# First loads of a four-layer attention kernel issued from two queues instead of one

## The chip, the core and the metric

The kernel runs on one core of a Trainium2 chip. Five engines work side by side and meet through semaphores: TensorE (PE in the profile, with its weight loads as PEld), VectorE (DVE), ScalarE (ACT), GpSimd (POOL) and SyncE (SP). Transfers between HBM and the core's memory are issued by an engine's sequencer (SPq, ACTq in the profile) and carried out by 16 DMA engines. The metric is device time in microseconds of one execution; lower is better.

## The reference

`x` is 2048 tokens of 512 values in bf16. Four residual layers follow each other, A, B, A, B. Only A's beginning matters here.

```python
def _A_ref(x, wqkv, w_phi, wo):                 # H = 32 heads of Dh = 16
    q, k, v = split_heads(x @ wqkv)
    pq = einsum("bhsd,hdf->bhsf", q, w_phi)     # one 16x16 matrix for each head
    pk = einsum("bhsd,hdf->bhsf", k, w_phi)
    phi_q = concat([softmax(pq), softmax(-pq)])
    phi_k = concat([softmax(pk), softmax(-pk)])
    kv  = einsum("bhsf,bhsd->bhfd", phi_k, v);  z = phi_k.sum over s
    num = einsum("bhqf,bhfd->bhqd", phi_q, kv)
    den = einsum("bhqf,bhf->bhq", phi_q, z) + 1e-6
    return merge_heads(num / den) @ wo

def _B_ref(x, wqkv, wo):                        # 8 earlier tokens at a stride of 2
    ...

x = x + _A_ref(layernorm(x), A_wqkv, A_w_phi, A_wo)
x = x + _B_ref(layernorm(x), B_wqkv, B_wo)
x = x + _A_ref(layernorm(x), A_wqkv, A_w_phi, A_wo)
x = x + _B_ref(layernorm(x), B_wqkv, B_wo)
```

## The kernel before

The tokens lie in four blocks of 512 (`x[0]` to `x[3]`, x0 to x3 in the text), each of four tiles of 128 tokens. All weights are held on the core. The matrices of `w_phi` are multiplied into the q and k parts of `wqkv` once, at the start ("fold"), so that layer A's first products give `pq` and `pk` at once.

The kernel is written as many small steps, each for one engine. `_ORDER`, a list of numbers, says which step is played next, and every engine then runs its instructions in that order; a solver made the list, and the tables of buffers (`_SLOTS`) with it. An engine that waits for something holds up everything behind it in its own order.

The head, up to about 14 us, is this:

- `s_loads` issues the loads. The four tiles of x0 come one by one (`lx0`, L337), x1 to x3 whole (`lx`, L340). The third part of `wqkv`, for v, goes straight to `WA` (`lv`, L343). The k and q parts go to raw buffers, `wraw`, each in two halves of 256 columns (`lraw`, L349); `qk` is 1 for k and 0 for q, `h` is the half. Then come pieces of the output weights `WoA` (L353), and layer B's `WB` and `WoB` (L418, L422). All of these are issued by SP. `w_phi` (`phis`, L325) is issued by ACT in `setup`, ahead of all steps.
- A DMA signals one of eight semaphores, handed out in turn in the order of the list over both queues. So a DMA's issue waits until the one eight before it has landed, and what stands behind it on that engine waits too.
- `s_fold`: PE transposes half of a raw part with eight products against the identity (`tr`, L386), DVE or ACT copies the result to `wT` (L202 is the copy on DVE, L204 on ACT), PE multiplies it with the block-diagonal `PHI` (`mm`, L396: 16 products of 128 columns for each part), and ACT copies four results to `WA` (L204, "CAST WA"). The part for k comes first, that for q after it.
- LayerNorm of x0: statistics of a tile on DVE (L515, L516), logarithm and exponential on ACT (L450, L453), the shift on DVE (L457, `nmr`), the tile itself on ACT (L468) or DVE (L466), transposes on PE (L482), copies on ACT.
- Then layer A's dense products: L632 for k (four products of 512 columns that add up, one for each row block of `WA`, so the fourth needs the last of the four casts), L644 for v, L737 for q; ACT takes exponentials from their results (L638 `Ek`, L745 `Eq`).
- `warm` (L309): products of a zero tile with itself, whose result nobody reads. Eleven come first on PE, two after the transposes of the first half of k, one after the transposes of the first tile of x0.
- `c_ind_av` (L268, `indAV`) is one of several small constants that DVE makes at the start.

On PE the order of the head is: eleven products of zeros; transposes of the first half of k; two products of zeros; transposes of the second half of k; transposes of x0's first tile; one product of zeros; transposes of the first half of q; then L396 for k with x0's second tile among them; transposes of the second half of q; L632.

Of the kernel before, what the change touches and what calls it, by code (L numbers as in the profile page):

```python
# [23 lines left out]
NB = 4  # L24
# [20 lines left out]
    "fold_dma": (),  # L45
    "half_k": ((0, 3), (1, 3)),
# [5 lines left out]
    "warm": 14,  # L52
# [8 lines left out]
8 2 i 2e 2p 23 i a i i 9 i i i i i i i 4e 1m i 0 0 f i e c j b 2 k 3 4 j o 1m l 3 m p 1n 0 i 1 n 1t o 1o q 1m 1p  # L61
r 0 1m 1u s 1m z z z 5 1m 1r 7 6 z 20 20 7 1q 1s 1t 21 21 t 20 20 1v 22 10 z 22 1t 7 1t 20 1w 22 t 11 24 24 13 u
12 16 12 1t t 15 1t v 12 12 22 x 18 14 1x d w w 1y 2c y 18 18 26 18 2d 1f 2d 2c 1z 2d 24 2d 27 17 19 18 1a 1b 21
1c 1d 22 21 22 39 1e 20 20 22 39 25 2c 3b 3a 3a 1f 3a 2d 3a 2f 2c 1f 1f 39 22 2f 2d 2g 1g 29 1f 2d 1j 2f 2d 7 1h
29 1i 1k 3a 29 2n 29 2i 2n 3c 2o 2o 2o 2k 2o 2k 2q 1l 2h 2n 2a 2k 2f 2n 2k 3a 2o 2j 24 2q 2r 2q 2o 2o 2o 29 2y
28 2y 2y 3c 2l 2z 2v 2z 2s 2z 2z 2k 2y 2z 39 36 31 2z 36 2z 3a 3b 36 36 2v 31 2v 37 2v 31 2t 36 2z 36 2b 2b 2b
2b 2m 2m 36 36 2m 3a 2w 2m 2v 33 34 32 31 3c 35 2q 3c 36 3b 2x g 2x 2u 2x 30 37 2x 36 38 38 38 38 3i 3c 3h 3c 39
3b 3a 3j 3k 3k 3k 3c 3d 3c 3e 3l 3b 3m 3d 3e 5h 3n 3m 3c 3e 3e 3l 5i 3o 3m 3q 3p 3m 3m 4f 3r 3m 3d 3l 5j 3e 3e
3s 3m 5i 3t 3m 3u 3m 3v 3d 3e 3e bd 5h 5m 5n 5k 5i 5l 5i 5i 3m 3d 3e 7c 5h 7d 5p 5i 5o 5i 5i 5r 3f 3g 3g 5q 5i
3f 3g 5i 3w 3f 3z 3x 3f 3g 5s 3y 7e 40 41 3g 7d 5u 5v 7f 5t 3g 41 42 41 41 44 3g 43 3g 43 5w 5x 5x 7f 45 46 43  # L70
43 47 43 7f 5y 3f 90 47 48 49 3g 4c 91 5x 41 4b 41 41 41 4a 92 5x 4d 60 91 4l 5z 61 5z 93 5z 4q 62 5z 4g 7d 4g
4g 4m 4q 63 5z 7d 4r 93 4i 4l 63 66 64 67 7g 4s 7j 65 7h 7i 4h 4j 7k bo 4n 4q 4q 4u 4w 91 7l 4t 7l 7l 7m 7l 7o
68 7n 7n 4l 7p 3h 7n 7q 4w 93 4v 7n 4v 91 4f 6a 7r 4o 6b 7n 6k 6f 69 4g 4k 4l 7r 6l 7s h 4w 6g 6k 6m 4p 6a 6c 6p
# [37 lines left out]

_SLOTS = {
    "med": (
        "b79ca642352f85de6b0464b12833892cb7516e70efd8561f1706ed4a53bc7430e3f9eba731d9c0411a4091d20483b8ae4cf4"
        "b71d6236f9ec40bfd6ea7830c4"
    ),
    "ps": (
# [19 lines left out]
class _Fast:  # L137
# [193 lines left out]
    def s_loads(self):  # L331
# [23 lines left out]
        for t in range(4):  # L355
            add("ld_x0", "SP", lx0, t)
# [1769 lines left out]
```

## Time and profile before

| | us |
|---|---|
| median of 3 runs | 319.39 (319.31 to 320.0) |
| profiled execution | 319.68 |
| its span | 317.9 |
| PE, DVE, ACT busy in the span | 307.5, 295.1, 275.2 |
| transfers, first 30 us | 6.87 MB, mean 229 GB/s |

In the profile's rows a group is given by line, engine, operation and output and input tiles. In the timeline the columns are start, length, engine, line, operation, and in brackets the engine's idle time just before and what ended it. In the rows of windows, the numbers after the stretch are its length and the busy time of PE, PEld, DVE, ACT and POOL with the count of instructions, then PE's granted clock, the DMA engines' share and GB/s. "To landing" is the time from a DMA's issue to its last semaphore increment. In the rows of DMA queues, q1 is SP's queue and q10 is ACT's; the columns are packets, MB and the time that the packets took as a share of 16 engines.

### The profile page before, as it was taken

Reading aid. Unit: us, or ns where it says so; the run is one execution under the profiler, and the core shown is the slowest. Engines: PE = TensorE matmul, PEld = TensorE weight load, DVE = VectorE, ACT = ScalarE, POOL = GpSimd, SP = SyncE. Lnnn points to the kernel's source line nnn. Section 1 sums busy time; section 2 is a strip of 40 time slices with the busy share of each in tenths; the row PEclk is TensorE's granted clock in tenths of the full one; section 3 lists DMA queues with packets and bytes.
Section 4 is the critical chain, followed back from the end, with each engine's and each line's share of the span. In section 5 each row is a group of like instructions: output and inputs, shape, how many; then the busy total and the mean of one; then the engine's idle time right before and its main releaser. Section 6 shows DMA issues by size and latency. Waiting matters only on the chain.

```text
span 317.9 us, 8896 instructions
## 1 busy us (share of the span) xinstructions
PE 307.5 (97%) x3578; PEld 153.0 (48%) x3578; DVE 295.1 (93%) x459; ACT 275.2 (87%) x639; POOL 47.1 (15%) x60
## 2 busy tenths in 40 slices
PE   8999999899999999999999999988999999999994
PEld 4654456445454444444444455544454544444552
DVE  6999996898999999999999999699998999999994
ACT  3999999999888778999999999899999867788761
POOL 6000000000003212000000000027011644045000
PEclk9999999999999999999999999999999999999999
DMA  6986200005694989569895500005189885565954
GB/s 199 345 203 143 41 2 4 2 19 142 150 191 96 157 141 139 99 106 151 140 131 71 69 0 2 4 19 134 49 195 137 134 157 119 103 181 122 163 148 170
DMA packets 45789, 36.37 MB, mean 114 GB/s; under 512 B 30832, under 2 KB 41136, under 8 KB 45744
## 3 DMA queue, kind: packets, MB, share of 16 engines
q1 hardware_dynamic: 45216, 35.75, 56.5%
q8 instruction: 29, 0.48, 0.7%
q14 instruction: 16, 0.13, 0.2%
q10 hardware_dynamic: 528, 0.02, 0.1%
HBM read 11.13 MB, written 3.25 MB: 45 GB/s over the span
## 4 chain that ended last, share of the span: by engine, by line
PE 88%; ACT 5%; DVE 2%; DMA 2%; SPq 1%; issue 1%; DVEq 0%; ACTq 0%
PE PS L967 23%; PE PS L553 18%; PE PS L632 9%; PE PS L644 9%; PE PS L737 6%; PE PS L1128 4%; PE PS L1066 4%; PE PS L1185 2%; DMA wraw<-in_A_wqkv_dram 2%; PE PS L707 2%; ACT Eq L745 2%; PE PS L482 1%; PE PS L940 1%; PE PS L556 1%; PE PS L1200 1%; PE PS L1082 1%
## 5 line engine op out<-in xcount | busy, mean ns | idle before, releaser
L967 PE MATMUL PS<-xnT,WB 128*128 128x512 bf16 x336 | 76.6, 380 | 0.0
L1059 DVE TENSOR_TENSOR prod<-QT,K 128x4096 bf16<-128x4096 bf16 x28 | 63.3, 2285 | 0.5 <-POOL K L993 0.5
L1121 DVE TENSOR_TENSOR pav<-PT,Vg 128x4096 bf16<-128x4096 bf16 (+1 forms) x29 | 62.9, 2213 | 0.2
L967 PEld LDWEIGHTS <-WB 128*128 128x128 bf16 x336 | 37.3, 114 | 36.3 <-issue 3.1
L745 ACT ACTIVATE Eq<-PS 128x512 bf16<-128x512 f32 x64 | 36.3, 619 | 0.0
L638 ACT ACTIVATE Ek<-PS 128x512 bf16<-128x512 f32 x64 | 35.1, 623 | 0.2 <-PE PS L632 0.2
L553 PEld LDWEIGHTS <-oT 128*128 128x128 bf16 x236 | 21.9, 98 | 26.6 <-issue 1.3
L737 PE MATMUL PS<-xnT,WA 128*128 128x512 bf16 x128 | 32.0, 380 | 0.5 <-DVE s L829 0.3
L578 ACT ACTIVATE sqd<-x 128x512 bf16<-128x512 bf16 x48 | 30.0, 635 | 2.1 <-DVE x L571 2.0
L644 PE MATMUL PS<-WA,xnT 128*128 128x512 bf16 x128 | 31.6, 379 | 0.0
L571 DVE SCALAR_TENSOR_TENSOR x<-PS,x 128x512 bf16<-128x512 f32 x46 | 30.1, 683 | 0.7 <-PE PS L553 0.7
L632 PE MATMUL PS<-WA,xnT 128*128 128x512 bf16 x128 | 30.7, 379 | 0.0
L204 ACT CAST oT<-PS 128x512 bf16<-128x512 f32 (+1 forms) x50 | 26.8, 600 | 3.6 <-PE PS L1128 2.1
L553 PE MATMUL PS<-WoA,oT 128*128 128x512 bf16 x128 | 29.8, 380 | 0.0
L553 PE MATMUL PS<-WoB,oT 128*128 128x512 bf16 x108 | 26.5, 379 | 0.0
L204 ACT CAST K<-PS 128x512 bf16<-128x512 f32 x30 | 17.3, 594 | 3.0 <-PE PS L967 1.9
L632 PEld LDWEIGHTS <-xnT 128*128 128x128 bf16 x128 | 12.4, 98 | 14.8 <-issue 0.4
L644 PEld LDWEIGHTS <-xnT 128*128 128x128 bf16 x128 | 12.3, 98 | 14.4 <-issue 0.4
L690 DVE TENSOR_TENSOR Ek<-Ek,rk 128x4096 bf16<-128x4096 bf16 (+1 forms) x10 | 18.6, 1859 | 0.4 <-ACT rk L685 0.4
L737 PEld LDWEIGHTS <-WA 128*128 128x128 bf16 x128 | 11.7, 98 | 14.6 <-issue 1.7
L466 DVE TENSOR_SCALAR xn<-x,rstd,nmr 128x512 bf16<-128x512 bf16 x48 | 17.5, 412 | 0.5
L204 ACT CAST V<-PS 128x512 bf16<-128x512 f32 x26 | 15.2, 596 | 2.9 <-PE PS L967 2.9
(175 smaller groups left out, 506.4 us busy)
## 6 DMA issues: line engine op xcount, KB each, us to landing
Vg<-V SPq DMA_DIRECT2D x112, 131.5 KB, 4.7
Prho<-rd SPq DMA_DIRECT2D x8, 512.0 KB, 5.3
x<-in_A_x_dram SPq DMA_DIRECT2D x3, 512.0 KB, 6.8
WB<-in_B_wqkv_dram SPq DMA_DIRECT2D x3, 512.0 KB, 9.6
out_dram<-x SPq DMA_DIRECT2D x6, 256.0 KB, 2.3
wraw<-in_A_wqkv_dram SPq DMA_DIRECT2D x4, 256.0 KB, 4.2
vd<-Vs SPq DMA_DIRECT2D x2, 272.0 KB, 3.0
x<-in_A_x_dram SPq DMA_DIRECT2D x4, 128.0 KB, 3.6
```

Source lines behind the costliest of these rows:

```text
L204: self.nc.scalar.copy(out=out, in_=in_)
L553: nc.tensor.matmul(y[:], lhsT=lh(t, c), rhs=Wo()[:, c, :], start=(c == 0), stop=(c == NB - 1 and not onpe))
L571: nc.vector.scalar_tensor_tensor(out=xb[:, t, :], in0=T[t][:], scalar=1.0, in1=xb[:, t, :], op0=ALU.mult, op1=ALU.add, **kw)
L578: nc.scalar.activation(out=sqd[:], in_=xb[:, t, :], func=ACT.Square, accum_out=T["ss"][:, t:t + 1])
L632: nc.tensor.matmul(pk[:], lhsT=xnT[:, t, k, :], rhs=self.WA[:, k, D:2 * D], start=(k == 0), stop=(k == NB - 1))
L638: nc.scalar.activation(out=T["E"][:, t, s, :], in_=T["k", t][:], func=ACT.Exp, scale=1.0 - 2.0 * s)
L644: nc.tensor.matmul(pv[:], lhsT=xnT[:, t, k, :], rhs=self.WA[:, k, 2 * D:3 * D], start=(k == 0), stop=(k == NB - 1))
L737: nc.tensor.matmul(pq[:], lhsT=self.WA[:, k, hb * P:(hb + 1) * P], rhs=xnT[:, :, k, :], start=(k == 0), stop=(k == NB - 1))
L745: nc.scalar.activation(out=self.Eq[L, b][s][:, :, hb, :], in_=T[hb][:].rearrange("p (t i) -> p t i", t=4), func=ACT.Exp, scale=1.0 - 2.0 * s)
L967: nc.tensor.matmul(pp[:], lhsT=self.WB[:, k, i * D + c:(i + 1) * D:NB], rhs=xnT[:, :, k, :], start=(k == 0), stop=(k == NB - 1))
L1059: nc.vector.tensor_tensor(out=pr[:], in0=QT[:, c:c + 1, :].to_broadcast([P, NW, TB]), in1=win, op=ALU.mult)
L1121: nc.vector.tensor_tensor(out=pv, in0=PT[:, :, lo:lo + n].unsqueeze(1).to_broadcast([P, NB, 2, n]), in1=vw, op=ALU.mult)
```

## The change

Four loads are issued by ACT instead of SP or ahead of the steps: x0's first tile, `phis` (now a step of its own, behind that tile), and two of the four halves of the raw parts: the second half of k and the first half of q (`raw_act`). `warm` goes from fourteen products to nine, all in one row at the start of PE. With it come a new `_ORDER` and new buffer tables.

```diff
+    "raw_act": ((1, 1), (0, 0)),
...
-    "warm": 14,
+    "warm": 9,
...
-        with nc.allow_non_contiguous_dma(reason="tiny w_phi load"):
-            nc.scalar.dma_start(out=self.phis[:], in_=self.A_w_phi.rearrange("(hb hl) d f -> (hl d) hb f", hb=NB))
...
+        def lphi():
+            with nc.allow_non_contiguous_dma(reason="tiny w_phi load"):
+                nc.scalar.dma_start(out=self.phis[:], in_=self.A_w_phi.rearrange("(hb hl) d f -> (hl d) hb f", hb=NB))
+
         def lx0(t):
-            nc.sync.dma_start(out=self.x[0][:, t, :], in_=xv[:, t, :])
+            q = nc.scalar if t == 0 else nc.sync
+            q.dma_start(out=self.x[0][:, t, :], in_=xv[:, t, :])
...
             c = qk * D + h * 256
-            nc.sync.dma_start(out=self.wraw[qk][:, :, h * 256:(h + 1) * 256], in_=wav[:, :, c:c + 256])
+            q = nc.scalar if (qk, h) in _OPT["raw_act"] else nc.sync
+            q.dma_start(out=self.wraw[qk][:, :, h * 256:(h + 1) * 256], in_=wav[:, :, c:c + 256])
...
         for t in range(4):
-            add("ld_x0", "SP", lx0, t)
+            add("ld_x0", "SP" if t else "ACT", lx0, t)
+        add("ld_phi", "ACT", lphi)
         add("ld_v", "SP", lv)
         for qk in (1, 0):
             if qk not in _OPT["fold_dma"]:
                 for h in range(2):
-                    add("ld_raw%d" % qk, "SP", lraw, qk, h)
+                    add("ld_raw%d" % qk, "ACT" if (qk, h) in _OPT["raw_act"] else "SP", lraw, qk, h)
...
 _ORDER = """
-8 2 i 2e 2p 23 i a i i 9 i i i i i i i 4e 1m i 0 0 f i e c j b 2 k 3 4 j o 1m l 3 m p 1n 0 i 1 n 1t o 1o q 1m 1p
+0 4 2 1 5 6 8 b 7 c m m e m m 27 m m d m 2t 4i m m i g 2i 1q n f o 1q n j s p q t 1r 1 3 r 1x s 1s u 1q 1t v 1
```

The added lines move the kernel's own line numbers by one to six.

SP's loads at the start, before. `wraw_138` is the k part and `wraw_192` the q part, each in its two halves; `x0_83` and `x1_84` are the first two blocks of x.

```order
L349 DMA wraw_138<-in_A_wqkv_dram 128x4x256
L337 DMA x0_83<-in_A_x_dram 128x512 x2
L349 DMA wraw_138<-in_A_wqkv_dram 128x4x256
L349 DMA wraw_192<-in_A_wqkv_dram 128x4x256
L340 DMA x1_84<-in_A_x_dram 128x4x512
L349 DMA wraw_192<-in_A_wqkv_dram 128x4x256
L337 DMA x0_83<-in_A_x_dram 128x512
L343 DMA WA_78<-in_A_wqkv_dram 128x4x512
```

And now, where `wraw_137` is the k part and `wraw_142` the q part:

```order
L354 DMA wraw_137<-in_A_wqkv_dram 128x4x256
L341 DMA x0_83<-in_A_x_dram 128x512
L344 DMA x1_84<-in_A_x_dram 128x4x512
L358 DMA WoA_79<-in_A_wo_dram 32x4x512
L354 DMA wraw_142<-in_A_wqkv_dram 128x4x256
L341 DMA x0_83<-in_A_x_dram 128x512
L347 DMA WA_78<-in_A_wqkv_dram 128x4x512
```

x1 has moved from sixth to third place and a piece of `WoA` comes right behind it; the second half of q stays behind both.

ACT's start, before (its next instruction after these is LayerNorm of tile 0):

```order
L317 ACT_TABLE_LOAD
L325 DMA phis_82<-in_A_w_phi_dram 128x4x16
L450 ACTIVATE lnv_188<-mv_183,eps_t_94 128x1
L453 ACTIVATE rstd_190<-lnv_188 128x1
L468 ACTIVATE xn_209<-x0_83,nmr_195,rstd_190 128x512
```

And now:

```order
L318 ACT_TABLE_LOAD
L341 DMA x0_83<-in_A_x_dram 128x512
L337 DMA phis_82<-in_A_w_phi_dram 128x4x16
L354 DMA wraw_137<-in_A_wqkv_dram 128x4x256
L354 DMA wraw_142<-in_A_wqkv_dram 128x4x256
L456 ACTIVATE lnv_188<-mv_184,eps_t_93 128x1
```

Tile 0 of x0 is ahead of `phis`, and the second half of k and the first half of q follow, all ahead of ACT's first arithmetic.

DVE's row from its constants to the second tile's statistics, before:

```order
L268 TENSOR_REDUCE indAV<-ident 128x32
L268 TENSOR_REDUCE indQK<-ident 128x32
L279 MEMSET indS 128x64
L281 COPY indS<-maskH 128x8 x4
L515 BN_STATS stat<-x_83 128x6
L516 BN_AGGR mv<-stat 128x2
L274 TENSOR_TENSOR PHI<-phis,maskH 128x512
L457 SCALAR_TENSOR_TENSOR nmr<-mv,rstd 128x1
```

And now:

```order
L269 TENSOR_REDUCE indQK<-ident 128x32
L280 MEMSET indS 128x64
L282 COPY indS<-maskH 128x8 x4
L521 BN_STATS stat<-x_83 128x6
L522 BN_AGGR mv<-stat 128x2
L275 TENSOR_TENSOR PHI<-phis,maskH 128x512
L463 SCALAR_TENSOR_TENSOR nmr<-mv,rstd 128x1
L269 TENSOR_REDUCE indAV<-ident 128x32
```

`indAV` has moved from before the first statistics to behind `nmr`, right ahead of the second tile's statistics. On PE the products of zeros between the transposes are gone and the rest of the head keeps its order up to L632. Behind it, four of L396's products for q stand four products later, and at two places near 22 to 26 us a group of four products of L737 changes places with one of L632 or L644. On ACT one reciprocal for `Ek` (`rk`) comes ahead of three `Ek`. On SP two more pieces of `WoB` come ahead of the first DMA transpose of `xn`.

More of the change, by code (lines that the diff above doesn't have):

```diff
@@ L101 @@
+fl ik gf ij ik gk ik gp gw gi gw fk ik go gf gt gx gv gv gv gx ge gj il il ij ik ij ik dy gv ij ij gw il dy ik
+dz gx im gx e0 fh ik in in im io gy gy in dy gx dy in e2 io il gy fi gw e3 ip gz fm gz im in in iq io ip fn fo
+fn e1 ir fp iu fn iv fn e1 fs iu fq iw im h0 h0 in gz ip in h1 io h0 ip is gz gz fr fq j2 h3 iu it iu iy ix h2
+iz ix h6 h0 h4 h0 h6 j3 h7 h8 h9 h7 h5 h6 ha h7 h6 h7 h9 hb h9 hc j2 h9 j4
 """
@@ L113 @@
     "med": (
[L114 removed]
+        "b6c9a742352f85de6b0464b12833892cb7516e70efd8561f1706ed4a53bc7430e3f9eba731d9c0411a4091d20483b8ae4cf4"
         "b71d6236f9ec40bfd6ea7830c4"
```

76 lines of the change are left out of this document (36 added, 40 removed).

## The prediction

> **What bounds the kernel now.** I read the page first, then the chain of waits in order of time, then the timeline of the first 14 us on each engine, then the landings and the windows of the transfers.
>
> ```profile
> span 317.9 us, 8896 instructions
> PE 307.5 (97%) x3578; PEld 153.0 (48%) x3578; DVE 295.1 (93%) x459; ACT 275.2 (87%) x639; POOL 47.1 (15%) x60
> PE 88%; ACT 5%; DVE 2%; DMA 2%; SPq 1%; issue 1%; DVEq 0%; ACTq 0%
> ```
>
> PE ends last and holds 88% of the chain; the 2% of DMA is one wait, in the head. The chain in order of time:
>
> ```profile
> 3.46 0.51 SPq L340
> 3.97 0.04 issue
> 4.01 6.41 DMA wraw<-in_A_wqkv_dram
> 10.43 0.05 issue
> 10.47 0.62 PE PS L386 x8
> 11.10 1.73 PE PS L632 x8
> ```
>
> SP issues one load after the other, the last quarter of `wraw` (call the quarters w10, w11, w00, w01 by `qk` and `h`) lands at 4.01 + 6.41 = 10.42, PE transposes it at 10.47, and from there the chain runs on PE without a hole (eight 512-column products in 1.73 us, 216 ns each) until 44.86. So a microsecond at this place is a microsecond at the end, unless something else takes the start. PE, ACT and DVE before it:
>
> ```profile
> 1.34 4.88 PE L309 MATMUL PS<-kvT 128*128 128x512 bf16 x11 [1.34 <-DVE kvT L264]
> 6.63 0.59 PE L309 MATMUL PS<-kvT 128*128 128x512 bf16 x2
> 7.95 0.61 PE L386 MATMUL PS<-ident,wraw 128*128 128x128 bf16 x8
> 8.39 0.39 PE L396 MATMUL PS<-PHI,wT 128*128 128x128 bf16 x4
> 9.01 0.83 PE L396 MATMUL PS<-PHI,wT 128*128 128x128 bf16 x12
> 10.47 0.62 PE L386 MATMUL PS<-ident,wraw 128*128 128x128 bf16 x8 [0.63 <-DMA wraw<-in_A_wqkv_dram]
> 8.82 0.59 ACT L204 CAST WA<-PS 128x512 bf16<-128x512 f32 x1 [0.30 <-PE PS L396]
> 9.78 1.58 ACT L204 CAST WA<-PS 128x512 bf16<-128x512 f32 x3
> 11.21 1.07 ACT L204 COPY wT<-PS 128x1024 bf16<-128x1024 bf16 x1
> 4.56 0.69 DVE L515 BATCH_NORM_STATS2 stat<-x 128x6 f32<-128x512 bf16 x1 [1.75 <-DMA x<-in_A_x_dram]
> 6.14 0.69 DVE L515 BATCH_NORM_STATS2 stat<-x 128x6 f32<-128x512 bf16 x1
> 7.72 0.69 DVE L202 COPY wT<-PS 128x1024 bf16<-128x1024 bf16 x1
> 13.65 0.69 DVE L515 BATCH_NORM_STATS2 stat<-x 128x6 f32<-128x512 bf16 x1
> ```
>
> There are two near-equal starts. PE waits 0.63 us for w01. But ACT is already full: its first cast (8.82) waits for L396, which stands on PE behind the transposes of w00 (7.95), and needs DVE's copy that ends at 8.41; DVE in turn has run without a hole since the first tile of x landed at 4.56. The last of the four casts ends at 11.36, and the fourth product of L632 needs it at 11.10 + 3 x 0.216 = 11.75. So there are only 0.39 us between ACT's start and PE's. Afterwards neither has room:
>
> ```profile
> 8.82:20.00 11.18, 10.55 (x95) 6.51 (x96) 10.59 (x30) 10.97 (x24) 0.00 (x0) 1.00 1.10 333
> 20.00:44.86 24.86, 24.86 (x122) 11.15 (x120) 24.04 (x44) 24.60 (x54) 0.54 (x1) 1.00 0.35 75
> 44.86:62.00 17.14, 15.66 (x520) 10.21 (x524) 13.21 (x26) 16.24 (x35) 0.47 (x2) 1.00 0.01 3
> ```
>
> After the stretch's length these rows give PE, PEld, DVE, ACT. ACT stands idle 0.21 + 0.26 us up to 44.86, where PE is full. A late ACT makes the end late but for about 0.47 us.
>
> **The change, part by part.** *The loads on two queues.* What decides is when w00 lands, because w00's transposes stand on PE ahead of every L396. Landings of before (issue, then time to landing):
>
> ```profile
> L349 SPq DMA_DIRECT2D wraw<-in_A_wqkv_dram x1: 455/455/455, 0.9 to 0.9; - x1
> DMA to landing us min/median/max: 3.2/3.2/3.2
> L349 SPq DMA_DIRECT2D wraw<-in_A_wqkv_dram x1: 507/507/507, 2.9 to 2.9; - x1
> DMA to landing us min/median/max: 4.3/4.3/4.3
> L340 SPq DMA_DIRECT2D x<-in_A_x_dram x1: 507/507/507, 3.5 to 3.5; - x1
> DMA to landing us min/median/max: 6.1/6.1/6.1
> 0.91 0.48 ACTq L325 DMA_DIRECT2D phis<-in_A_w_phi_dram  x1
> ```
>
> These are w10 (issued 0.92, landed 4.1), w00 (issued 2.92, landed 7.2, 0.7 us before PE came to it) and x1, the second 512 KB of x (issued 3.46, landed 9.6). On one queue they go in order. Both sequencers need about half a microsecond for an issue (0.48 for `phis` on ACT's) and start at 0.9. Now w00 is fourth on ACT's queue, at about 2.4, while SP's queue issues x1 third, at about 1.9, and WoA behind it. How do two queues share? Before shows it once, when the small load `phis` (ACT's queue, q10) met w10 (SP's, q1). The windows 2.6 to 3.4, then two where SP's queue was alone (5.2 to 5.7 with 512-byte packets, 11 to 12 with 1 KB ones), then the page's count of `phis` packets and the window of 4.0 to 5.0, whose row ends in the share of the DMA engines and GB/s:
>
> ```profile
> q1 hardware_dynamic: 399, 0.21, 86.5%
> q10 hardware_dynamic: 419, 0.01, 29.4%
> q1 hardware_dynamic: 314, 0.16, 106.7%
> q1 hardware_dynamic: 388, 0.38, 108.3%
> q10 hardware_dynamic: 528, 0.02, 0.1%
> 4.00:5.00 1.00, 1.00 (x4) 0.33 (x3) 0.44 (x1) 0.00 (x0) 0.78 (x4) 1.00 0.63 182
> ```
>
> 399 packets against 419 in the same 0.8 us, but 0.21 MB against 0.01: the queues take turns by packets, not by bytes and not by issue. Alone, each of 16 engines takes 16 x 500 / 314 = 25 ns for 512 bytes and 16 x 1000 / 388 = 41 ns for 1 KB. So, per engine, a quarter of wraw (32 packets) costs 0.82 us, a tile of x 0.33 (8 packets of 1 KB), x1 1.32 (32), the first WoA 0.33 (8), and phis 0.30 (29.4% of 0.8 us for 419 of its 528).
>
> In turns, ACT's first 41 packets (tile 0 of x, phis) pass beside SP's first 40 (w10, tile 1 of x); then w11's 32 beside x1's 32; then w00's 32 beside WoA's 8 and 24 of w01. Work done when w00 is through: 0.82 + 0.33 + 0.33 + 0.30 + 0.82 + 1.32 + 0.82 + 0.33 + 0.62 = 5.69 us. Before, on one queue, w00 was through after 3.42 (without x1, WoA and w01) and landed at 7.2; x1 after 4.74, and landed at 9.6. The quicker issue gains back the hole at 4.0 to 5.0, share 0.63, so 0.37 us. From w00's row: 7.2 + (5.69 - 3.42) - 0.37 = 9.1. From x1's: 9.6 + (5.69 - 4.74) - 0.37 = 10.2. I take 9.45, nearer the first, because it is the same load with the same packets; x1's row has its own late stragglers. Both ends stay for the range. Even if the queues shared by bytes, about the set that x1 needed before would pass first (4.74): 7.2 + 1.32 - 0.37 = 8.2 or, by x1's own row, 9.2.
>
> The Trainium skill (DMA: Bandwidth & Descriptors, "Issuing engines are not separate DMA queues") says that loads issued from several engines run on the same 16 DMA engines and interleave, and that this saves the sequencer's issue time only. By that rule the gain would be at most the hole, 0.37 us; the two-queue rows agree.
>
> PE then starts w00 at 9.45 instead of 7.95, 1.5 us late, and with it L396, the casts and ACT's whole stream. PE itself: 1.89 us from there to the end of L396 (7.95 to 9.84), so w01's transposes come at 11.34 instead of 10.47, +0.87; the fourth product of L632 waits for the last cast, +1.5 less the spare 0.39 = +1.1. ACT: +1.5 less 0.47 = +1.0. I take **+1.1 us**.
>
> *w01* is fifth on SP and, as every DMA here, waits for the one eight before it, w10, to land (4.1 before, perhaps 4.8 now); behind it on SP stand tile 2 of x, WA's third part, tile 3. Its packets have x1's in front, so the later issue costs nothing; total work is 0.33 more (WoA), less the hole: 10.4 +/- 0.4, behind the new PE time of 11.34. Tile 3 of x now waits for x1 to land; DVE takes up its last tile only at 13.65.
>
> *Tile 0 of x first on ACT*: issued at about 0.9 instead of 1.42; sharing with w10 it lands between 4.05 and 4.55. DVE's chain gains 0 to 0.5, and loses the 0.36 of `indAV` (L268), moved from DVE's idle time before 4.56 into the chain behind it. Net -0.5 to +0.3, near 0; hidden behind the late w00, and what counts if w00 is not late.
>
> *Five products fewer*: two of the first eleven (4.88 / 11 = 0.44 us each) and three between the transposes (0.59 for two). All lie where PE then waits for landings or for DVE's copies: 0. That cover is w11 and w00; with both early, DVE's copy at 7.72 is next.
>
> *Moves elsewhere*: two more WoB ahead of the first DMA transpose on SP.
>
> ```profile
> SPq L473 <- DVE xn L466: 8.4, 2, 6.7
> ```
>
> SP waits 6.7 us there for DVE, which covers two issues more. Groups of four products of L737, L644 and L396 change places on PE, one `rk` comes before three `Ek` on ACT: the same work on full engines, 0, with +/- 0.3 for the waits that they may open (0.30 us is what ACT's waits of this kind took at 8.82).
>
> Sum: +1.1. The profiled execution took 319.68 (span 317.9 and 1.8 around it), 0.3 above the median of 319.39. It becomes 320.8, the median **320.5**.
>
> **Rivals.** *A, w00 is on time: not slower.* If ACT's queue gets ahead (x1's 512 packets ready later than w00's), w00 lands by 7.2. It decides at 7.95 + 0.39: landing by 8.3, the end does not move. For it speaks that x1 is issued only about as early as w11; against it the two-queue rows and the byte bound of 8.2 to 9.2. Then DVE's chain (up to -0.5) and w01 (10.0 to 10.4, so up to -0.4) set the start: 318.9 to 319.5, likeliest 319.2. To get below 318.75 it takes both at their best, and the reordering (up to 0.3) on top.
>
> *B, late but soaked up.* w00 at 8.2 to 8.8: +0 to +0.45, 319.4 to 319.9.
>
> *C, PE's clock.* The first eleven products took 444 ns each, the later ones of the chain 216. With nine and then two waits of about a microsecond, PE may still, or again, run slowly when it gets dense: eight products then cost 1.73 more, and a slow stretch of 3.4 us costs 1.7. Added to the forecast 322.2, alone 321.1. Against it: PE is busy from 1.34 to about 6 without a hole as before. The Trainium skill (TensorE: Matmul & The Clock Gate, "The HAM clock gate") says that the clock opens after about 3.4 us of sustained work and closes after an idle window as long; by that rule the nine products (4 us) are enough.
>
> **Numbers.** The forecast (w00 at 9.1 to 10.2: 320.1 to 321.3; with the moves its own range is 319.9 to 321.5) has 0.53, A 0.23, B 0.15, C 0.09. From 318.8 to 321.8 leaves out about one in ten on each side: A at its best with the reordering below, C on top of the forecast above. A measurement of this kernel tells from no change about 0.2%, 0.64 us. Faster: A's part below 318.75, 0.11. Same: the rest of A, B and a sliver of the forecast, 0.28. Slower: the forecast and C, 0.61.
>
> **What would show it.** Right: the transposes of w00 wait on a DMA of `wraw` until after 9, the first cast of WA starts past 10, the wait before the last quarter is gone or small, L632 starts near 12.2, x1 lands before w00. Wrong: w00's transposes at 8 or earlier, ACT's first cast at or before 8.8, or L632 before 11. Clock: 8 dense products over 1.73 us after 11.

## The result: slower, and by more than forecast

The change takes 323.36 us (median of 6 runs, 321.65 to 324.77) against 319.41 us (319.31 to 320.0) for the kernel before in the same comparison: ratio 1.0114 with a 95% interval of 1.0081 to 1.0148. In a later comparison it was 323.33 against 319.65, ratio 1.0109 [1.0092, 1.0126]. The forecast was 320.5, in a range of 318.8 to 321.8: the direction was right, and the time came out 2.9 us above the forecast and 1.6 us above its range.

The profiled execution took 322.68 us, span 321.0. The page's lines, in the order in which those of before were shown, with the slices of PE's clock (its granted clock in tenths of full speed, in 40 equal slices of the span) between them:

```profile
span 321.0 us, 8884 instructions
PE 307.4 (96%) x3573; PEld 153.5 (48%) x3573; DVE 295.6 (92%) x459; ACT 275.1 (86%) x639; POOL 47.0 (15%) x60
PEclk9799999999999999999999999999999999999998
PE 79%; ACT 11%; DVE 4%; DMA 2%; issue 2%; ACTq 0%; DVEq 0%
```

All engines have the same busy time as before within 0.5 us. PE is as long busy with five products of zeros fewer, so some of its work took longer; for the rest the 3.1 us longer span is waiting. PE's share of the chain falls from 88% to 79%; ACT has 11%. The second slice of PEclk reads 7: the clock was not full there. The chain in order of time (start, length, what):

```profile
2.40 7.93 DMA wraw<-in_A_wqkv_dram
10.33 0.05 issue
10.38 1.03 PE PS L392 x8
11.41 0.43 PE PS L402 x4
11.84 0.25 PE PS L488 x4
12.10 0.68 PE PS L402 x12
12.78 0.06 issue
12.84 1.58 ACT WA L205 x3
```

The load that decides is now w00, issued at 2.40 and landed at 10.33, not w01. Behind it the chain goes over L402 (L396 before) into ACT's casts, not over L632. The timeline of PE, then of ACT, then of DVE:

```profile
1.34 3.88 PE L310 MATMUL PS<-kvT 128*128 128x512 bf16 x9 [1.34 <-DVE kvT L265]
5.06 0.61 PE L392 MATMUL PS<-ident,wraw 128*128 128x128 bf16 x8
8.40 1.03 PE L392 MATMUL PS<-ident,wraw 128*128 128x128 bf16 x8 [2.73 <-DMA wraw<-in_A_wqkv_dram]
10.38 1.03 PE L392 MATMUL PS<-ident,wraw 128*128 128x128 bf16 x8 [0.53 <-DMA wraw<-in_A_wqkv_dram]
11.21 0.63 PE L402 MATMUL PS<-PHI,wT 128*128 128x128 bf16 x4
13.00 0.61 PE L392 MATMUL PS<-ident,wraw 128*128 128x128 bf16 x8 [0.24 <-ACT xnT L205]
...
11.88 0.58 ACT L205 CAST WA<-PS 128x512 bf16<-128x512 f32 x1 [1.40 <-PE PS L402]
...
3.28 0.69 DVE L521 BATCH_NORM_STATS2 stat<-x 128x6 f32<-128x512 bf16 x1 [0.75 <-DMA x<-in_A_x_dram]
5.01 0.69 DVE L275 TENSOR_TENSOR PHI<-phis,maskH 128x512 bf16<-128x512 bf16 x1 [0.82 <-DMA phis<-in_A_w_phi_dram]
```

PE waits 2.73 us for w11 and 0.53 for w00. The transposes of w00 start at 10.38 instead of 7.95 (+2.43), ACT's first cast at 11.88 instead of 8.82 (+3.06). Behind the cast the same instructions are 2.7 to 2.8 us late up to 30 us, and 2.9 to 3.3 us from 45 us to the end. The 0.63 between the first two numbers is in PE's work itself: eight transposes took 1.03 us instead of 0.61, and the four products of L402 behind them 0.63 instead of 0.39. The windows say why (PE's granted clock is the third number from the end):

```profile
8.00:9.00 1.00, 0.60 (x6) 0.61 (x7) 0.00 (x0) 0.00 (x0) 0.00 (x0) 0.68 1.17 277
9.00:10.00 1.00, 0.85 (x9) 0.59 (x6) 0.54 (x1) 0.11 (x1) 0.00 (x0) 0.50 1.11 331
10.00:11.00 1.00, 0.62 (x7) 0.62 (x8) 0.48 (x2) 0.48 (x1) 0.00 (x0) 0.50 0.99 304
11.00:12.00 1.00, 1.00 (x14) 1.00 (x13) 0.55 (x1) 0.12 (x1) 0.00 (x0) 0.61 0.81 223
12.00:13.00 1.00, 0.77 (x14) 0.65 (x12) 0.96 (x4) 1.00 (x3) 0.00 (x0) 1.00 0.94 323
```

From 8.36 to 11.78 the clock was half. So two things in the head are to be told apart: late loads, and a halved clock. A third comes later. Between 30 and 34 us the new order has ACT take the first reciprocal for `Ek` (it begins with L690, L684 before) three `Ek` earlier than before; ACT now waits there for DVE's sum `s`, and did not before:

```profile
31.93 0.44 ACT L684 ACTIVATE s<-s 128x256 f32<-128x256 f32 x1
33.80 0.42 ACT L690 ACTIVATE s<-s 128x256 f32<-128x256 f32 x1 [0.46 <-DVE s L684]
```

The first of these rows is from before, the second from the change. The landings of the two loads that ACT issues at 1.8 and 2.4 (least is w11, most is w00):

```profile
L354 ACTq DMA_DIRECT2D wraw<-in_A_wqkv_dram x2: 528/528/529, 1.8 to 2.4; - x2
DMA to landing us min/median/max: 6.5/7.2/7.9
```

### The profile page after: what moved, and what is told of

Read it like the earlier page. It is cut to its first block, busy times and chain, and to the rows that moved or that the text cites. A ratio compares the mean times of both kernels' runs of the same rounds, so it can differ in the third digit from the quotient of the medians.

```text
span 321.0 us, 8884 instructions
## 1 busy us (share of the span) xinstructions
PE 307.4 (96%) x3573; PEld 153.5 (48%) x3573; DVE 295.6 (92%) x459; ACT 275.1 (86%) x639; POOL 47.0 (15%) x60
## 3 DMA queue, kind: packets, MB, share of 16 engines
HBM read 11.13 MB, written 3.25 MB: 45 GB/s over the span
## 4 chain that ended last, share of the span: by engine, by line
PE 79%; ACT 11%; DVE 4%; DMA 2%; issue 2%; ACTq 0%; DVEq 0%
PE PS L973 23%; PE PS L559 17%; PE PS L650 6%; PE PS L638 6%; PE PS L743 5%; PE PS L1072 4%; PE PS L1134 4%; ACT Eq L751 3%; DMA wraw<-in_A_wqkv_dram 2%; ACT Ek L644 2%; PE PS L1191 2%; PE PS L713 2%; PE PS L946 1%; ACT WA L205 1%; PE PS L1206 1%
## 5 line engine op out<-in xcount | busy, mean ns | idle before, releaser
L644 ACT ACTIVATE Ek<-PS 128x512 bf16<-128x512 f32 x64 | 35.3, 625 | 0.2 <-PE PS L638 0.2
L638 PE MATMUL PS<-WA,xnT 128*128 128x512 bf16 x128 | 30.9, 379 | 0.3
L638 PEld LDWEIGHTS <-xnT 128*128 128x128 bf16 x128 | 12.3, 98 | 15.6 <-issue 1.7
L650 PEld LDWEIGHTS <-xnT 128*128 128x128 bf16 x128 | 12.2, 98 | 14.2 <-issue 0.4
```

Of the source, the lines that this page charges most:

```text
L638: nc.tensor.matmul(pk[:], lhsT=xnT[:, t, k, :], rhs=self.WA[:, k, D:2 * D], start=(k == 0), stop=(k == NB - 1))
L644: nc.scalar.activation(out=T["E"][:, t, s, :], in_=T["k", t][:], func=ACT.Exp, scale=1.0 - 2.0 * s)
L650: nc.tensor.matmul(pv[:], lhsT=xnT[:, t, k, :], rhs=self.WA[:, k, 2 * D:3 * D], start=(k == 0), stop=(k == NB - 1))
```

## The experiments

Each kernel is compared with the kernel before on its own chip. "First cast" and "end" are given against the trace of before (8.82 and 317.85), transposes of w00 against 7.95; "the body" is by how much the same instructions between the head and 280 us come later than in before. The trace of an experiment is one of its runs, and not always a typical one.

**The halves back on SP's queue.** The change with all four quarters of `wraw` on SP; the order of steps stays, so x1 and WoA come behind w00.

```diff
-            q = nc.scalar if (qk, h) in _OPT["raw_act"] else nc.sync
+            q = nc.sync
```

> The change with its two halves of wraw issued by SP again, in the change's own order of steps; ACT keeps tile 0 of x and phis. Theory S (two queues share each DMA engine in turns, so w11 and w00 are slowed by x1 and WoA beside them): on one queue w11 and w00 are ahead of x1 again, w00 lands at about 7.2 (10.3 in the change), its transposes start near 8, PE's clock does not fall, and the time is 319.4 +/- 0.5. Rival T (the new order of steps and the nine products of zeros are what costs): 322 to 323.5, as in the change. Rival L (loads on ACT's queue are slow in themselves, whatever runs beside them): as S for wraw, but tile 0 and phis land no earlier than in the change (3.25 and 5.0).

320.24 us, ratio 1.0024 [1.0006, 1.0042]. w00 landed at 7.17; PE waits for DVE there, not for a load, and the first cast is where it was:

```profile
7.69 0.61 PE L392 MATMUL PS<-ident,wraw 128*128 128x128 bf16 x8 [0.42 <-DVE wT L203]
8.79 0.58 ACT L205 CAST WA<-PS 128x512 bf16<-128x512 f32 x1 [0.70 <-PE PS L402]
```

So about four fifths of the loss hangs on where the two halves are issued. What stays of the change (the new order and tables, nine products, tile 0 and `phis` on ACT) costs 0.2 to 1.3 us by the interval; the time lies above the 319.4 +/- 0.5 expected. The trace shows one place for it: the first cast is 0.03 early, the body is 0.3 early up to 30 us and 0.2 late from 45 us on, and between them ACT waits 0.47 us for `s` ahead of the reciprocal. In the seven traces with the new order this wait is 0.19 to 0.47 us; no trace with the old order has it.

**Products of zeros in PE's waits.** The change with eight more: six ahead of w11's transposes, two ahead of w00's (eight more steps in `_ORDER`, left out here).

```diff
-    "warm": 9,
+    "warm": 17,
```

> The change with eight products of zeros put into PE's two waits (six before the transposes of w11, two before those of w00), seventeen in all. Theory C (PE's clock is halved for one or two windows of 3.4 us because PE stands idle for 2.7 us, and this makes up about 0.6 us of the profiled loss and all the spread from 321.7 to 324.8): the granted clock stays full through 14 us, the spread falls under 0.5 us, and the time is 321.5 to 322.3, since the late landing of w00 (about 2.4 us) stays. Rival S alone (only the landing counts): the time is that of the change, 323.4, or more. Rival P (the products are in the way of the transposes): 324 and over.

322.54 us (321.39 to 323.71), ratio 1.009 [1.0064, 1.0116]: about 0.8 less than the change, though the two intervals overlap, and the spread of 2.3 us remains; 321.5 to 322.3 and a spread under 0.5 were expected. With w00 landing at 10.02 the eight transposes take 0.62 again:

```profile
6.01 2.12 PE L308 MATMUL PS<-kvT 128*128 128x512 bf16 x6
10.06 0.62 PE L390 MATMUL PS<-ident,wraw 128*128 128x128 bf16 x8 [0.84 <-DMA wraw<-in_A_wqkv_dram]
10.95 0.58 ACT L203 CAST WA<-PS 128x512 bf16<-128x512 f32 x1 [1.53 <-PE PS L400]
```

The granted clock of these six runs is 0.995 to 1.0, and 2.9 us of loss remain, 1.8 more than forecast. So by this kernel the clock is the smaller part of the loss; the larger part and most of this spread come without it. In the trace the body is 1.8 late up to 30 us and 2.3 from 45 us on.

**Nine products in the kernel before.**

```diff
-    "warm": 14,
+    "warm": 9,
```

> The kernel before with nine products of zeros at the start instead of fourteen, nothing else. Theory S+C: the loads come as before, PE's waits are under a microsecond, the clock stays full from 6 us on: 319.4 +/- 0.4. Rival T (the missing products cost by themselves): 321 or more, with a fall of the granted clock before 12 us.

All nine stand at the start. 319.44 us, ratio 0.9992 [0.998, 1.0004]: alone the missing products cost nothing.

**The split alone.** The kernel before, w11 and w00 on ACT's queue behind `phis`, the issue of w00 ahead of the first tile's logarithm on ACT.

```diff
+            q = nc.scalar if (qk, h) in ((1, 1), (0, 0)) else nc.sync
...
-... b 2 k 3 4 j ...
+... b 2 3 k 4 j ...
```

> The kernel before, with its order, buffers and fourteen products of zeros, and only the halves w11 and w00 issued by ACT behind phis (w00's step moved ahead of ACT's first logarithm, so that it is issued at once). Theory S: w00 meets x1 and w01 in turns and lands at 8.5 to 10.5 instead of 7.2; its transposes start 0.5 to 2.5 us later than 7.95; the time is 320 to 322, with PE's clock mostly full thanks to the fillers. Rival T (order and tables cost, not the queues): 319.4 +/- 0.4 or better. Rival F (two queues feed faster): w00 lands before 7.2 and the time is below 319.2.

319.64 us, ratio 0.9998 [0.9989, 1.0006]: harmless, where theory S had expected 320 to 322. w00 was issued at 2.1 and landed 5.7 us later, at 7.76, in time for PE at 7.86; the first cast came at 8.97. Its rows for w11 and w00:

```profile
L348 ACTq DMA_DIRECT2D wraw<-in_A_wqkv_dram x2: 528/570/612, 1.4 to 2.1; - x2
DMA to landing us min/median/max: 4.1/4.9/5.7
```

Here x1 was issued at 2.44, behind w00's issue at 2.05; in the change it is issued at 1.97, ahead of w00's at 2.40, and WoA at 2.44 besides. So two queues as such cost nothing here. That what stands beside w11 and w00 costs is the reading that the next two test; w00 is also issued 0.35 earlier here than in the change, since tile 0 is not on ACT.

**x1 later, two queues.** The change with x1 (step 8) and WoA (b) behind w01 (7) on SP.

```diff
-0 4 2 1 5 6 8 b 7 c ...
+0 4 2 1 5 6 7 8 b c ...
```

> The change with one thing altered: on SP's queue x1 and the first piece of WoA come behind the last quarter of wraw (w01), so that x1 is issued after w00 and not beside w11. ACT's queue is as in the change. Theory (the queues serve about in order of issue, and the 512 packets of x1 that SP issued at 1.97 us, ahead of w00, are what made w11 and w00 late): w00 lands at 8.3 us or earlier, its transposes start within 0.5 us of 7.95, first cast of WA at 8.8 to 9.4, time 319.4 to 320.2, and the runs lie within 1 us of each other. Rival (two queues are slow whatever stands on SP, or ACT's longer list is at fault): w00 after 9.3, time 322 to 323.5 with a spread as in the change.

321.21 us (320.81 to 322.68), ratio 1.0048 [1.0035, 1.0061]: less than half the loss, but not the 319.4 to 320.2 that the theory wanted. w01 now passes in x1's place, and x1, issued at 2.44, still beside w00; the sum by turns, made as in the prediction, is 5.56 us of work for w00 against 5.69 in the change and 5.18 in the split alone.

**x1 earlier, one queue.** The kernel before, x1 ahead of w11.

```diff
-... b 2 k 3 4 j ...
+... b 4 2 k 3 j ...
```

> The kernel before, all on SP's queue, with one load moved: x1 is issued ahead of the second half of k (w11). Theory (x1's place ahead of w11 and w00 is what costs, with one queue or two): w11 lands near 7.8, w00 near 8.5 to 9.0, so the first cast is 0.9 to 1.4 late and the time is 320.3 to 320.9. Rival (on one queue the place of x1 is harmless, only the meeting of two queues costs): 319.4 within 0.3.

321.01 us (320.52 to 323.37), ratio 1.0052 [1.0034, 1.0069]. The place of x1 costs on one queue too. In the trace w11 came at 9.45, later than the 7.8 expected, and the clock was halved behind it (1.03 us for eight transposes). The traced runs of both are the slowest of their kind (322.68 and 323.37), so their rows show a bad case. The wait of PE in each of the two, x1 late and x1 early:

```profile
9.73 1.03 PE L390 MATMUL PS<-ident,wraw 128*128 128x128 bf16 x8 [1.60 <-DMA wraw<-in_A_wqkv_dram]
```

```profile
9.50 1.03 PE L384 MATMUL PS<-ident,wraw 128*128 128x128 bf16 x8 [2.78 <-DMA wraw<-in_A_wqkv_dram]
```

**The change twice more**, one run each with a trace.

> The change once more, unaltered, for a second trace. Theory (w00's landing is set by the slowest of the 16 DMA engines, and the granted clock falls to half for one stretch of 3.4 us whose place differs from run to run): w11 and w00 land more than 1 us later than before, but not at the same times as in the first trace (8.35 and 10.33), within about 1 us of them; the halved stretch starts at another place, between 7 and 11 us, and the time lies between 321.6 and 324.8. Rival (both are fixed): the same landings within 0.2 us and the same stretch.

> The change once more, for a third trace. Theory (every run of the change has w00 landing at 9.3 to 10.6, its place set by the slowest DMA engine, and one or two stretches of 3.4 us at half clock): time 321.6 to 324.8; the later end equals the later first cast within 0.3 us. Rival (the end is late by something else than the head): the end is later by 0.5 us or more than the first cast is.

321.87 and 321.81 us. w00 landed at 9.37 and 9.12. In the second of these traces the clock stayed full through the head:

```profile
9.17 0.62 PE L392 MATMUL PS<-ident,wraw 128*128 128x128 bf16 x8 [1.71 <-DMA wraw<-in_A_wqkv_dram]
10.05 0.58 ACT L205 CAST WA<-PS 128x512 bf16<-128x512 f32 x1 [1.76 <-PE PS L402]
```

Transposes +1.22, first cast +1.23, the body +0.9 up to 30 us: this is the forecast's mechanism, with the spare of about 0.3 that it counted on. Then the reciprocal of the new order waits 0.46 us, and the body is +1.45 from 45 to 287 us. The end is +2.23, against the expectation of 0.3 between cast and end: another 0.8 opens up between 287 and 300. About 0.5 of it stands ahead of PE's first product with `Vx`: it starts 0.09 us behind the last landing of the loads `Vx<-vd` (294.08 and 293.99; 292.16 and 292.07 in before), and PE's wait for it is 0.68 us, 0.21 in before. The traces of the products of zeros (+0.64) and of the loads alone in their last comparison (+0.70) lose at the same product, others less or nothing; why these loads land later there stays open. In the first of the two traces w11 landed at 6.46, 1.9 earlier than in the change's first trace, and the clock was half from 8.92 to 12.33, the first cast +2.10 with transposes +1.47: 0.63 for the clock again.

**The loads alone.** The kernel before with the change's loads, and nothing else. The first try left w00's step (3) behind the first tile's logarithm (k) on ACT:

```diff
-... b 2 k 3 4 j ...
+... b 2 k 3 4 7 j ...
```

> The kernel before, with its fourteen products of zeros and its order of everything that is not a load, but with the change's loads: ACT issues x0's first tile, phis, w11, w00; SP issues w10, x0's second tile, x1, the first piece of WoA, w01. Theory (the loads carry the loss: w00 late by its turns with x1 and WoA and by the slowest DMA engine, and then the halved clock): transposes of w00 at 9.3 to 10.4, time 322 to 323.4, in some runs a granted clock of 0.995 or less. Rival (the new order of the other steps or the missing products are part of it): 320.5 or less.

325.88 us, ratio 1.0182 [1.0164, 1.0201]: a miss, by a wait that the change does not have. w00's issue was given the semaphore of w11 and waited until w11 had landed at 8.92; the normalised tile, queued behind it on ACT, waited as well:

```profile
8.95 0.37 ACTq L350 DMA_DIRECT2D wraw<-in_A_wqkv_dram  x1
9.43 0.81 ACT L469 ACTIVATE xn<-x,nmr,rstd 128x512 bf16<-128x512 bf16 x1 [4.37 <-DMA wraw<-in_A_wqkv_dram]
```

So semaphores do not simply go round in the order of the list, as the section on the kernel has it: a load that stands behind a waiting step can get one that is still in use. With the step ahead:

```diff
-... b 2 k 3 4 7 j ...
+... b 2 3 4 7 k j ...
```

> The kernel before with its fourteen products of zeros and its order of everything but the loads, which stand as in the change, w00's issue now straight behind w11's on ACT. Theory (the loads carry the loss): w00 lands at 9.1 to 10.4, first cast 1.2 to 3 us late, time 320.9 to 323.4. Rival (the new order of the other steps carries part of it): w00 lands as late, but the time is 320.5 or less; or w00 lands by 8.3.

320.94 us (320.32 to 323.66), ratio 1.0048 [1.0029, 1.0067]. w00 landed at 9.29:

```profile
9.34 0.62 PE L387 MATMUL PS<-ident,wraw 128*128 128x128 bf16 x8 [1.57 <-DMA wraw<-in_A_wqkv_dram]
10.22 0.58 ACT L202 CAST WA<-PS 128x512 bf16<-128x512 f32 x1 [2.04 <-PE PS L397]
```

Transposes +1.39, first cast +1.40, the body +1.1 to +1.2, the end +1.16. This trace is the prediction's sum for the loads (1.5 late, 1.1 at the end) almost to the tenth, and the ratio gives 1.5 us. On this chip the loads cost little more than was forecast for them; on the chip of the next three they cost 2.2 us, so the close agreement of this trace is in part luck.

**Loads, zeros and order on one chip.**

The three kernels that follow ran on one chip ("the common chip" below). First the loads alone again, the kernel of the last experiment, as the measure (e18 in the texts):

> The loads of the change with the fourteen products and the old order, once more, as the measure for the other two. Both theories: 320.5 to 321.5, clock above 0.996 in most runs.

Then the same with nine products in one row at the start, the steps in their old order (e17):

```diff
-    "warm": 14,
+    "warm": 9,
```

> The kernel before with the loads of the change and nine products of zeros, everything else in its old order. Theory (without the products between the transposes PE stands idle long enough while it waits for w11 and w00 that the clock falls): 322 to 323.6 and a clock below 0.997 in most runs, 1 us or more above e18. Rival (the products count for nothing, as they did without the late loads; the new order makes the rest): 320.5 to 321.3, as e18.

Then the change itself, with the new order too (e16):

> The change, unaltered, on the chip of the next two. Theory (loads late by 1.2 to 1.5 us, and on top the clock at half for one stretch, or two, of 3.4 us in most runs): 322 to 323.6, granted clock 0.989 to 0.997. Rival (the rest was the chip of the first comparison): as e18 within 0.5 us.

| loads of the change, and | us | ratio to 319.65 | granted clock of the runs |
|---|---|---|---|
| 14 products, old order | 322.01 (320.42 to 323.23) | 1.0070 [1.0046, 1.0093] | 0.995 to 1.0 |
| 9 products, old order | 323.20 (321.16 to 324.12) | 1.0102 [1.0077, 1.0126] | 0.987 to 0.999, four of six below 0.990 |
| 9 products, new order | 323.33 (321.67 to 323.75) | 1.0109 [1.0092, 1.0126] | 0.989 to 1.0 |

The loads cost 0.7% here (2.2 us, where 320.5 to 321.5 had been expected for the time), the five products 0.3% on top (1.0 us); from the second row to the third there are 0.1 us more. The intervals overlap from row to row, so no step is sharp; that the middle one is one, the clocks say, and the 0.4 us that the new order costs in the traces is less than these rows can show. The five products, free in the kernel before, cost about a microsecond once the loads are late. In the trace with fourteen products w00 landed at 10.21, not at 9.29 as on the other chip, with the clock full:

```profile
10.26 0.62 PE L387 MATMUL PS<-ident,wraw 128*128 128x128 bf16 x8 [0.68 <-DMA wraw<-in_A_wqkv_dram]
```

Transposes +2.31, first cast +2.32, the body +2.1, the end +2.83. The trace with nine products and the old order had two stretches at half clock in a row:

```profile
10.34 1.04 PE L387 MATMUL PS<-ident,wraw 128*128 128x128 bf16 x8 [2.12 <-DMA wraw<-in_A_wqkv_dram]
11.84 0.59 ACT L202 CAST WA<-PS 128x512 bf16<-128x512 f32 x1 [3.00 <-PE PS L397]
```

Transposes +2.39, first cast +3.02, the body +4.1.

**Four tries at a faster head**, from the kernel before, with w11 and w00 on ACT. The first two edits are shown against the kernel before, the last two each against the try ahead of it. The first issues x0's first tile ahead of w10 and x1 ahead of w01, and has DVE copy w10 ahead of the second tile's statistics (o):

```diff
-8 2 i ... i 0 0 f ... b 2 k 3 4 j o 1m l 3 m p 1n 0 i 1 n 1t o 1o q 1m 1p r ...
+8 0 2 i ... i 0 f ... b 2 3 k 4 j 1m l 3 m 1n o p 0 i 1 n o 1o q 1m 1p 1m 1t r ...
```

> A try at a faster head, from the kernel before with its fourteen products of zeros: SP issues x0's first tile ahead of w10, then x0's second tile, x1 and w01; ACT issues phis, w11, w00; on DVE the copy of w10's transposes comes ahead of the second tile's statistics, and PE transposes w00 after the first half of k's products. Theory (VectorE's row from the first tile of x0 on sets the first cast, and w00 lands by 8.3): first cast 0.5 to 0.6 earlier than before, near 8.2, L632 at 10.1 to 10.5, time 318.7 to 319.1. Rival (w11 or w00 comes late, since x1 stands ahead on SP, or w01's landing at 10.4 sets L632 anyway): 319.3 to 320.5.

The second issues two tiles of x0 first, leaves DVE's order as it was, and has two products of zeros fewer (twelve):

```diff
-8 2 i ... 4e 1m i 0 0 f i e c j b 2 k 3 4 j o 1m l 3 m ... n 1t o 1o q 1m 1p r ...
+8 0 0 2 i ... 4e 1m f e c j b 2 k 3 j o 1m l 3 4 m ... n o 1o q 1m 1p 1m 1t r ...
```

> A second try at a faster head, with VectorE's order left as before, which the first try had spoilt. SP issues two tiles of x0, w10, w01, x1; ACT issues phis, w11, w00; the two products of zeros between the transposes of the k half are left out, and PE transposes w00 behind the first eight products with PHI. Theory (VectorE's row from the first tile on sets the first cast): first cast 8.2 to 8.5, so 0.3 to 0.6 earlier than before, L632 at 10.2 to 10.6, time 318.8 to 319.2. Rival (w00 lands after 8.3 or the gain is eaten by waits further on): 319.4 to 320.2.

The third puts w00's issue (3) ahead of the logarithm (k) and its transposes (1t) behind all products of k with `PHI`; the fourth puts DVE's copy of them (1u) behind the first statistics of x1 (z):

```diff
-... b 2 k 3 j ... 1m 1t r 0 1u s 1m z z z 5 1m 1r ...
+... b 2 3 k j ... 1m r 0 s 1m 1m 1t 1u z z z 5 1r ...
...
-... 1t 1u z z z 5 1r ...
+... 1t z 1u z z 5 1r ...
```

> The faster head once more: SP issues two tiles of x0, w10, w01, x1; ACT issues phis, w11, w00, now with w00 issued at about 1.9 instead of 4.98, and PE makes all products of k with PHI before it transposes w00. Theory (VectorE's row sets the first cast, w00 lands by 9): first cast near 8.3, last cast ends near 10.9, L632 at 10.1 to 10.5, time 318.7 to 319.2. Rival (w00 or w01 after 9.6, or the gain is lost in the waits behind): 319.4 to 320.5.

> The faster head with one thing put right: VectorE copies w00's transposes behind the first statistics of x1, not ahead of them, since it stood idle 1.40 us for them and ScalarE then 1.30 us for the statistics. Theory (that wait alone ate the gain): L632 at 9.6 to 10.2, the wait of ScalarE ahead of its logarithm of x1 0.5 us or less, time 318.9 to 319.5. Rival (the landings differ too much from run to run): 320 or more, with a spread above 1.5 us.

320.96 (ratio 1.0046 [1.0034, 1.0058]), 324.40 (1.0151 [1.0137, 1.0165]), 321.37 (1.0059 [1.004, 1.0078]) and 320.25 (1.0018 [1.0005, 1.0032]). None beats the kernel before, and none came out at the 318.7 to 319.5 that its theory expected. Each time the wait that was removed was followed by another: DVE's shift of the second tile, waiting for ACT ahead of the copy that the first cast needs; w00's issue held until 4.98, behind the same logarithm as above; ACT waiting for x1's statistics; and, in the last, w10's slowest engine (7.16, where 14 of 16 were through by 6.51). One row of each, in that order:

```profile
8.57 0.16 DVE L456 SCALAR_TENSOR_TENSOR nmr<-mv,rstd 128x1 f32<-128x1 f32 x1 [0.60 <-ACT rstd L452]
```

```profile
12.44 0.93 PE L385 MATMUL PS<-ident,wraw 128*128 128x128 bf16 x8 [3.98 <-DMA wraw<-in_A_wqkv_dram]
```

```profile
13.37 0.30 ACT L449 ACTIVATE lnv<-mv,eps_t 128x4 f32<-128x4 f32 x1 [1.30 <-DVE mv L515]
```

```profile
7.20 1.07 PE L385 MATMUL PS<-ident,wraw 128*128 128x128 bf16 x16 [0.98 <-DMA wraw<-in_A_wqkv_dram]
```

The expected first cast did come in the second and third (8.28 and 8.10 instead of 8.82), and L632 started 1.24 early in the third; the end was still +0.48, in the fastest of that kernel's runs (320.06). The runs of the last lie between 319.40 and 321.27, as its rival expected (the landings differ too much from run to run), and the traced one took 321.20.

## Why the prediction was right or wrong

The mechanism was right: w00 lands late beside x1, and PE, the casts and the end follow. The sum failed in three terms. The loads were put at +1.1 and cost 1.5 us on one chip and 2.2 on another. The five products of zeros were put at 0, with the clock left beside the sum as a rival; together with the late loads they cost about 1.0 us. The moves elsewhere were put at 0 +/- 0.3 and cost about 0.4. On the common chip the change cost 3.5 us by the ratio, 2.4 more than forecast; of these the loads make about 1.1 and the products about 1.0. Why the same loads cost 1.5 us on one chip and 2.2 on another stays open: on the common chip two engines lagged in two of the three traces and none in the third.

*w00's landing, 9.45 (9.1 to 10.2).* Near the middle, but not where a run lands. The four traces of the change have 10.33, 9.37, 9.12 and 8.97; four other traces with the same loads have 10.02 (products of zeros), 9.29, 10.21 and 10.30 (loads alone, twice, and with nine products). So four lie between 8.97 and 9.37 and four between 10.02 and 10.33, about where the forecast's two rows, 9.1 and 10.2, stood; taking 9.45 gave the late landings too little weight. The work by turns also puts one queue and the split alone ahead of the rest (w00 at 7.17 and 7.76, against 9.69 with x1 behind w01 and 9.0 to 10.3 with the change's loads), but gives too much for the split alone: 7.2 + (5.18 - 3.42) - 0.37 = 8.6 against 7.76. A likely reason, not tested by itself, is that x1 counted there as passing in turn from its first packet, though it was issued after w00. What the sum lacked is the spread of the 16 engines. The middle one finished w00 at 8.4 to 8.75 in all four traces of the change; the slowest, which lets PE start, 0.3 to 1.9 us later. A landing is a maximum over 16, and its price must be taken from the slow end.

*What passes through to the end, 1.1 of 1.5.* The spare was there: with the clock full the body up to 30 us is 0.3 less late than the first cast, with either order (0.9 of 1.23 in the change, 1.1 of 1.40 and 2.0 of 2.32 in the loads alone). So in the old order a landing at 9.29 costs 1.2 us from 45 us on, and one at 10.21 costs 2.1.

*Five products fewer: 0, and rival C, the clock: 0.09.* This step failed. Alone the products are free, as said; the text even named the condition ("That cover is w11 and w00"), but then put the products and the late loads into separate terms. Together they take PE's work out of one stretch: of 3.41 us ahead of the halving PE was busy 0.72. The argument against C, that PE is busy from 1.34 to about 6 as before, looked at the start, and was wrong there too (the zeros ended at 5.2); the clock fell in the later waits, where nothing stood between the transposes. C's price was fair for what it hits: 0.63 on the first cast for the part of one stretch in two traces, 1.7 on the body beyond the late transposes with two stretches. Its chance was not: of 13 runs of the change the granted clock was 0.995 or lower in 11, and in none of the 83 runs of the kernel before beside the experiments was it below 0.997. So C belongs in the forecast. It is not the whole rest: one run of the change took 323.35 at a clock of 1.0, and the products of zeros brought the time back by 0.8 us only.

*Moves elsewhere, 0 +/- 0.3.* The reciprocal that comes ahead of three `Ek` opens a wait of 0.19 to 0.47 us on ACT in every trace with the new order. For the same first cast the body behind 45 us is 0.4 later than in the old order: 0.2 above the first cast's delay instead of 0.2 below it, where the clock is full. That is a little above what the forecast allowed for such waits.

*The range.* It left C on top of the forecast (322.2) outside. A landing at the late end (10.2, +2.1 on the body in the trace with fourteen products on the common chip) and C (+0.6 to +1.7) give 322.1 to 323.2, just below the medians of 323.36 and 323.33; the moves would add 0.4.

*x0's first tile, -0.5 to +0.3.* It landed at 3.25 in the first trace, earlier than forecast, but `phis` behind it came at 4.99 instead of 4.30, and DVE waited 0.82 us for it ahead of `PHI`. Nothing was gained.

*w01.* It was issued only at 4.35, waiting for w10's semaphore, and landed at 11.03 in the first trace, later than 10.4 +/- 0.4; PE came to it at 13.00, so it did not count.

*Rival A*, w00 on time by 8.3, did not happen in any trace of the change; the split alone shows that it was possible with x1 issued after w00. Of the signs named: transposes of w00 waiting until after 9 (in three of the four traces clearly, at 9.02 in the fourth) and a first cast past 10 came; L632 (L638 now) came at 13.45, not near 12.2, from the landing at 10.33 instead of 9.45 and the clock, and at 11.62 in the trace with the full clock; x1 landed at 9.62, ahead of w00.

The rule of the Trainium skill quoted there (DMA: Bandwidth & Descriptors, "Issuing engines are not separate DMA queues") agrees with the traces: from 2 to 11 us the engines moved 2.64 MB before and 2.58 MB after.

## What to carry to other kernels

When first loads are spread over queues, look at what is issued beside and just before the load that the chain waits for: a large load with no hurry (x1) ahead of them costs on one queue (0.5%) as on two, and its place counted here for more than the second queue (0.9998 with x1 issued after w00). Fillers on PE that are free while loads are early hold the clock when they are late, so removing them and delaying loads must be costed together. In a list of steps, a load's issue must stand ahead of any step that waits on the same engine. When a step is moved forward on a full engine, as the reciprocal is here, the arrival of its input has to be timed too.

## What the runs showed of the hardware

*In these traces the clock follows stretches of 3.41 us, and how full each is.* In the records of the clock it changes only on a grid of 3.413 us, whose phase differs from run to run. In 22 stretches at full clock in the heads of these traces, PE's busy time decides the next one: the eight with 0.15 to 1.56 us were followed by half clock, the fourteen with 1.72 us or more by full clock. The stretch before the halving in the change's first trace and in its fourth, then two in a row in the first try at the loads alone, of which the second was followed by half clock (PE's busy time is the second number behind the stretch):

```profile
4.95:8.36 3.41, 0.72 (x9) 0.43 (x7) 2.55 (x7) 1.31 (x3) 1.72 (x10) 1.00 1.06 305
```

```profile
5.94:9.35 3.41, 1.56 (x21) 1.02 (x20) 2.97 (x9) 1.79 (x4) 0.80 (x4) 1.00 1.15 308
```

```profile
4.69:8.10 3.41, 1.72 (x14) 0.84 (x12) 2.12 (x5) 0.34 (x2) 1.91 (x10) 1.00 1.07 295
8.10:11.51 3.41, 1.23 (x13) 0.73 (x13) 0.82 (x3) 1.79 (x4) 0.00 (x0) 1.00 1.00 308
```

The Trainium skill (TensorE: Matmul & The Clock Gate, "The HAM clock gate") has the window of 3413 ns running free, which agrees, and an idle window as the condition for half clock; here a window with PE busy 46% of it (1.56 of 3.41) was enough, and the traces decide. With waits of about that size, the phase of the grid decides, and that is likely a part of the spread from 321.7 to 324.8.

The way back takes more. Of ten halved stretches in these heads, the eight with PE busy 2.65 us or more were followed by full clock, and the two with 1.00 and 2.57 by another halved one. The latter is from the nine products with the old order:

```profile
9.50:12.91 3.41, 2.57 (x25) 2.58 (x26) 1.46 (x4) 1.07 (x2) 0.00 (x0) 0.50 0.98 316
```

One halved stretch takes 0.005 off the mean clock of some 320 us, two take 0.011. Of the runs of the change the five at a clock of 0.989 took 323.33 to 324.77 us, the five at 0.994 or 0.995 took 321.65 to 322.13. A later landing can lengthen the time and bring the second stretch as well, so these runs don't separate the two.

*The 16 engines of one load finish far apart.* w00's 256 KB in the change's first trace came in between 8.15 and 10.33: ten engines by 8.64, the last two at 9.93 and 10.33. In the loads alone on the common chip two engines are 1.2 us behind the rest (8.88, then 10.05 and 10.21); in the first try at the loads alone one engine brought w11 2.7 us behind the other fifteen (6.26, then 8.92). The Trainium skill (DMA: Bandwidth & Descriptors, "Why a DMA increments its semaphore by 16 and not by 1") says that the engines finish independently; which engine lags, and why, stays open. A head with no slack for it shows it in its runs: 321.65 to 324.77, against 319.31 to 320.0 for the kernel before, whose w00 landed 0.7 us ahead of its use.
